# Weight conversion in three phases, and row statistics and reciprocals moved from VectorE to ScalarE and GpSimd, in a top-k attention with an MLP

## The chip, the cores and the metric

The kernel runs on one core of one Trainium2 chip. The metric is device time in microseconds (us). Engines are named as in the profile: PE is TensorE, DVE is VectorE, ACT is ScalarE, POOL is GpSimd and SP is SyncE, which here only issues DMAs. Each engine works through its own instructions in order; waits between engines go by semaphores.

## The reference

Eight batches of eight heads, 576 positions, head width 64. Each row of attention keeps its 32 largest scores; the eight heads' results form rows of 512, which go through a layer norm without bias and a two-layer MLP with a residual.

```python
scores = scale * np.matmul(q, k.transpose(0, 1, 3, 2))
kth = np.partition(scores, -top_k, axis=-1)[..., -top_k:-top_k + 1]
scores = np.where(scores >= kth, scores, -1000000000.0)
attn = np.exp(scores - np.max(scores, axis=-1, keepdims=True))
attn = attn / (np.sum(attn, axis=-1, keepdims=True) + 1e-09)
x = np.matmul(attn, v)            # then (B,H,S,D) -> (B, S, H*D)

mu = np.mean(x, axis=-1, keepdims=True)
var = np.mean((x - mu) ** 2, axis=-1, keepdims=True)
xn = (x - mu) / np.sqrt(var + 1e-06) * g_ln
out = x + np.maximum(xn @ w_ch1, 0.0) @ w_ch2
```

q, k, v and g_ln come as 32-bit floats, the two weight matrices (512 x 2048 and 2048 x 512) as 64-bit floats. The kernel computes in 32 bits.

## The kernel before

**Units and steps.** A unit is 128 query rows of two heads (or the 64 last rows of two heads, a "rest" unit); there are 160. One pass of the loop `for n in range(END)` is a step. In step n different units are at different stages, so that every engine has work: PE makes the scores of unit n+2 and ACT copies them from PSUM (`scores`, `take_scores`, L433 and L414); DVE searches unit n for its 32nd largest score (`select`, L464, L470, L478) and halves unit n+1's rows (`halve`, L456, L457); ACT and POOL mask unit n-1 (`prepare` L490, L491; `mask` L527 on ACT, L530 on POOL), ACT takes its exponential with row sums (`weigh`, L538). Older units are transposed (PE and ACT, L601 to L641, or DVE and DMAs, `move`, L572 to L589) and multiplied with the values (`values`, L664, L672).

**Placing.** When a group's last unit is done, ACT copies the product (`take_values`, L682), PE transposes it, and `place` scales it by the reciprocal of the row sums (`put`, L686, four a group on ACT) into a row tile x. The reciprocal is made on DVE, one instruction for a group (L1350), after the second part of `select`, in the same step before L686. A step in which this happens is called a place step below.

**Blocks.** Two row tiles form a block; there are 18. `Block.stats` runs in the step after x is complete: DVE's two statistics instructions give mean and variance (L737, L738). For the first block DVE also subtracts the mean (L740); for the others POOL negates the mean (L743) and adds it (L746). `inverse` makes the reciprocal root on POOL (L756, and the power L759). PE transposes x (L775), multiplies with the first weight (L821, ACT's relu L844), then with the second (L860 for the first two blocks, L981 with seven products instead of eight for the others, whose sums POOL makes, L911 to L917). ACT evacuates (L946, L955) and scales (L796), POOL adds the residual (L789).

**Filling.** A block's PE work lies in the list `todo`. `fill`, called eight times a step, takes from it as much as a share worked out by `slot` allows, and also runs the delayed work (`Later.settle`, by age in calls of `fill`). `give` puts a new block's items into the list: its transposes stand ahead of the last ten items of the block before. An item is only taken when its condition holds: the transposes want x centred six calls ago.

**Weights.** 32 pieces of 128 x 512 64-bit numbers are fetched by SP (L148) into tiles of a ring of four that x also uses, and turned into 32-bit floats: ACT takes the size and the low word (L164, L166), POOL clamps and takes the sign (L165, L169), DVE shifts (L172), POOL adds (L178). `batches` says which pieces belong to which step: four before the first step, one a step for steps 0 to 7, none in step 8, one in step 9, two a step from 10 to 18, one in 19. For the early pieces the fetch comes a step ahead, the split in the middle of the step, the shift near its end, the join at the end of the next; from step 9 on the fetch comes at the end of the step before, the split in the middle, the shift near the end, the join near the start of the next.

Scratch in PSUM for scores, transposes and value products comes from a ring of five buffers (`brief`).

Of the kernel before, what the change touches and what calls it, by code (L numbers as in the profile page):

```python
# [9 lines left out]
AF = mybir.ActivationFunctionType  # L10
ALU = mybir.AluOpType
FP32 = mybir.dt.float32
# [8 lines left out]
LN_EPS = 1.0e-6  # L21
J = 4
# [7 lines left out]
def compute(  # L30
# [21 lines left out]
    scale = 1.0 / float(D) ** 0.5  # L52
# [4 lines left out]
    def pool(name, bufs, **kw):  # L57
        return ctx.enter_context(tc.tile_pool(name=name, bufs=bufs, **kw))
# [17 lines left out]
    brief_small = pool("brief_small", 2)  # L76
# [36 lines left out]
    columns = const([P, J + NC], "columns")  # L113
    half, gcol = columns[:, 0:J], columns[:, J : J + NC]
    nc.gpsimd.memset(half[:], -0.5)
    w1 = const([P, NC, DFF], "w1")
    w2 = const([P, NF, DM], "w2")
    wt = const([P, 2, NF // 2, 2 * P], "wt")
# [65 lines left out]
    now = [-1]  # L184
# [19 lines left out]
    LATE = NF // 2 + 1  # L204
# [25 lines left out]
    def done(step):  # L230
        return step is not None and step < now[0]

    def pop():
        kind, cost, run, may = todo.pop(0)
        assert not may or may()
        owed[0] -= cost
        run()

    tick = [0]
# [20 lines left out]
            for _, run in due_now:  # L260
                run()

    sums_later, ends_later, stores = Later(), Later(), Later()

    loads, sends = Later(), Later()
    brings = {}
# [1 line left out]
    def fill(least=0):  # L268
        tick[0] += 1
        loads.settle(LOAD_AGE)  # L270
        sends.settle(SEND_AGE)
        ends_later.settle(END_AGE)
        fetch_forms(FETCH_AGE)
# [185 lines left out]
    def select(u, i):  # L459

        nt = range(len(u.tiles))

        def replace(m, t, x):
            nc.vector.match_replace(x, m[:, t, :], x, LOWEST)  # L464

        if i == 1:
            for r in range(low_rounds):
                o = u.low + 8 * r
                for t in nt:
                    nc.vector.max(u.hi[:, t, o : o + 8], u.lo[:, t])  # L470
                if r < low_rounds - 1:
                    for t in nt:
                        replace(u.hi[:, :, o : o + 8], t, u.lo[:, t])
        r0, width = (min(u.low, u.body), HALF + LOWS) if i > 1 else (u.body, HALF)
        pl = brief_small if i in (1, 2) else small
        m = pl.tile([P, 2, 8], FP32, tag=f"m{i}", name=f"m{i}")
        for t in nt:
            nc.vector.max(m[:, t, :], u.hi[:, t, r0 : r0 + width])  # L478
# [242 lines left out]
    class Block:  # L721
# [9 lines left out]
        def stats(self, i):  # L731
            x = self.x[i]
            if self.mv is None:
                self.mv = small.tile([P, 2, 2], FP32, tag="mv", name="mv")
                self.rstd = small.tile([P, 2], FP32, tag="rstd", name="rstd")
            st = brief_small.tile([P, 6], FP32, tag="st", name="st")
            nc.vector.bn_stats(out=st[:], in_=x)  # L737
            nc.vector.bn_aggr(out=self.mv[:, i, :], in_=st[:])  # L738
            if now[0] <= gives_first:
                nc.vector.tensor_scalar_sub(x, x, self.mv[:, i, 0:1])  # L740
            else:
                less = brief_small.tile([P, 1], FP32, tag="less", name="less")
                nc.gpsimd.tensor_scalar(  # L743
                    less[:], self.mv[:, i, 0:1], -1.0, 0.0, ALU.mult, ALU.add
                )
                nc.gpsimd.tensor_scalar(x, x, 1.0, less[:], ALU.mult, ALU.add)  # L746
            self.step[i] = tick[0]

        def centred(self, i):
            return i in self.step and (  # L750
# [3 lines left out]
        def inverse(self):  # L754
            r = self.rstd[:, 0 : self.n]
            nc.gpsimd.tensor_scalar(  # L756
                r, self.mv[:, 0 : self.n, 1], 1.0, LN_EPS, ALU.mult, ALU.add
            )
            nc.gpsimd.tensor_tensor(r, r, half[:, 0 : self.n], ALU.pow)  # L759
            self.ready = True  # L760
# [250 lines left out]
    SEND_AGE, CENTRE_AGE = 1, 6  # L1011
# [38 lines left out]
    def fetch_form():  # L1050
        m = fetched[0]
        k, i = m // 4 % 2, m % 4
        nc.sync.dma_start(
            slot_of(i), scratch[:, k, i].rearrange("p (f n) -> p f n", f=2)
        )
        fetched[0] += 1

    def fetch_forms(age):
        if done(formed[0]):
            free = 4 + sum(tick[0] - x >= age for x in used)  # L1060
            while fetched[0] < min(free, 8 * (len(blocks) - PLAIN)):
                fetch_form()
# [57 lines left out]
    gives = {}  # L1120
# [9 lines left out]
    for j in jobs:  # L1130
        if j.hp == NHP - 1:
            b = j.b
# [26 lines left out]
    def at(i):  # L1159
        return units[i] if 0 <= i < N else None  # L1160
# [42 lines left out]
    def dve_cost(n):  # L1203
        u, ex = at(n), after(n)[0]
        c = 4.0 if u is None else DVE_REST if u.rest else DVE_UNIT
        if n <= CONVERTING:
            c += 1.0
        c += DVE_TURN * (n in turns) + 0.85 * sum(b.n for b in gives.get(n, []))
        return c + DVE_MOVE if ex and ex.moved else c

    def give(n):
# [36 lines left out]
    gives_first = min(gives)  # L1248
    load(fresh[0], nc.sync, nc.scalar)

    nc.scalar.copy(gcol[:], half[:])
    for x in batches[-1]:
        x.fetch()
    turn_heads(fresh[0])
    nc.sync.dma_start(grow[:], g_ln.rearrange("(c p) -> c p", p=P))
    scores(units[0])
# [3 lines left out]
    scores(units[1])  # L1260
    take_scores(units[1])
    load_gain()
    weights(-1, 0)
    weights(-1, 1)
    for n in range(END):
        now[0] = n
# [42 lines left out]
            brings.pop(n)()  # L1309
        if u:  # L1310
            select(u, 0)
        if n > NF // 2:
            join_weights(n)
# [25 lines left out]
        if ex and ex.rest:  # L1339
            keep_den(ex)  # L1340
        if u:
            select(u, 1)
        if moved:
            move(ex)
        if n == gives_first:
# [1 line left out]
                blk.stats(i)  # L1347
        sums_later.settle(SUM_AGE)
        for den in recips.pop(n, []):
            nc.vector.reciprocal(den, den)  # L1350
        if n in turns:
            turn_heads(turns[n])
            later = fresh.index(turns[n]) + 1
# [47 lines left out]
        if n == 0:  # L1401
            for x in batches[-1]:
                x.shift()
            for x in batches[-1][:2]:
                x.join()
        weights(n, 1)
        if 0 < n <= NF // 2:
            join_weights(n)
            for x in batches[-1][n + 1 : n + 2]:
                x.join()  # L1410
        if g and not quick and g.job.hp == NHP - 1:
            for qt in g.qts:
                if qt < J:
# [1 line left out]
        if late and late.job.hp == NHP - 1:  # L1415
            r = late.job.b // 2
# [62 lines left out]
```

## Time and profile before

| | |
|---|---|
| three runs, median | 1562.06 us (1561.92 to 1564.73) |
| the profiled execution's own time | 1566.49 us |
| its span | 1564.6 us |
| granted PE clock, mean | 0.971 |
| busy PE, DVE | 1467.7 us, 1349.1 us |
| busy ACT, POOL | 1075.5 us, 941.2 us |
| bytes moved by DMA | 245.62 MB |

The profile's page lists busy time by engine and the chain of work that ended last. Three kinds of answers from the trace are used beside it: busy time of each engine in a stretch of the span, waits (who waited for whom, us in total, how often, the longest), and groups of equal instructions (line, engine, operation, tiles, shapes, count, then busy us and mean ns of one, then idle time ahead of them and what ended it). A timeline row gives start and duration in us; what stands in brackets is the idle time of the engine ahead of it and what ended that. PE multiplies 32-bit numbers in two records for each product in the program.

### The profile page before, as it was taken

To read this page: it belongs to the slowest core of one execution; us is meant where nothing else is said; L and a number is where in the kernel's file an instruction comes from. 1 tells how busy PE (TensorE), PEld (TensorE's weight loads), DVE (VectorE), ACT (ScalarE), POOL (GpSimd) and SP (SyncE) were. 2 spreads that over 40 slices of the span, in tenths; PEclk is the share of its full clock that TensorE was granted. 3 is DMA by queue.
4 is the path that set the end of the run, shared out by engine and by line. 5 is a ranking of instruction groups with operands and counts; after the bars stand their busy time and mean duration, and the time that the engine had idled before them with its cause. 6 is when DMAs were issued, how large, how long until landed. Compare 5 with 4: busy or idle time off the path is not lost.

```text
span 1564.6 us, 27256 instructions
## 1 busy us (share of the span) xinstructions
PE 1467.7 (94%) x8046; PEld 1108.0 (71%) x8046; DVE 1349.1 (86%) x3873; ACT 1075.5 (69%) x3085; POOL 941.2 (60%) x1302
## 2 busy tenths in 40 slices
PE   3678889999999899999999999999999999999997
PEld 2456447576787677778777777777777777788886
DVE  6998899899889998989988999999999999767000
ACT  5988777786777767777777776867677776554421
POOL 4757776756474666656656556565647475737524
PEclk7789989999999999999999999999999999999998
DMA  6634541567648774686744796666667567464511
GB/s 174 165 100 122 143 114 60 151 157 209 177 127 201 192 204 130 180 207 151 222 119 133 183 225 183 159 171 182 187 173 197 173 173 196 118 173 114 151 35 50
DMA packets 374776, 245.62 MB, mean 157 GB/s; under 512 B 255956, under 2 KB 343512, under 8 KB 374616
## 3 DMA queue, kind: packets, MB, share of 16 engines
q1 hardware_dynamic: 371048, 243.17, 57.9%
q8 instruction: 67, 1.10, 0.3%
q10 hardware_dynamic: 3568, 0.59, 0.3%
q14 instruction: 93, 0.76, 0.2%
HBM read 166.14 MB, written 77.53 MB: 156 GB/s over the span
## 4 chain that ended last, share of the span: by engine, by line
PE 52%; DVE 31%; ACT 5%; DMA 5%; POOL 4%; issue 2%; SPq 1%; DVEq 0%; POOLq 0%; ACTq 0%
PE hps L821 21%; PE ops L981 13%; DVE m L478 10%; DVE hi L464 8%; PE scps L433 6%; PE av L664 5%; DVE sc L572 3%; DVE lo L457 2%; DVE hi L456 2%; PE ops L860 2%; DVE hi L470 2%; PE tp L601 2%; POOL e L530 2%; DMA raw<-in_moe_w_ch_dram 1%; PE av L672 1%
## 5 line engine op out<-in xcount | busy, mean ns | idle before, releaser
L530 POOL TENSOR_TENSOR e<-e,sc 128x576 f32<-128x576 f32 x288 | 408.7, 1437 | 492.6 <-ACT e L527 437.7
L821 PE MATMUL hps<-xT,w 128*128 128x256 f32 x2304 | 542.0, 384 | 1.6 <-ACT xT L781 1.6
L821 PEld LDWEIGHTS hps<-xT,w 128*128 128x128 f32 x2304 | 423.4, 191 | 80.8 <-issue 25.9
L478 DVE MAX8 m<-hi 128x8 f32<-128x296 f32 (+1 forms) x1152 | 472.8, 446 | 1.2
L464 DVE MATCH_REPLACE8 hi<-m,hi 128x288 f32<-128x288 f32 (+1 forms) x864 | 378.0, 443 | 0.0
L981 PE MATMUL ops<-w,h 128*128 128x256 f32 x1280 | 306.9, 385 | 1.3 <-ACT o L946 1.3
L981 PEld LDWEIGHTS ops<-w,h 128*128 128x128 f32 x1280 | 235.0, 191 | 44.8 <-issue 13.4
L414 ACT COPY sc<-scps 128x288 f32<-128x288 f32 x576 | 189.1, 402 | 76.8 <-POOL e L530 56.0
L538 ACT ACTIVATE e<-e,m 128x576 f32<-128x576 f32 x288 | 225.4, 785 | 7.8 <-POOL e L530 5.8
L527 ACT ACTIVATE e<-sc,m 128x576 f32<-128x576 f32 x288 | 209.3, 769 | 0.0
L572 DVE STREAM_TRANSPOSE sc<-e 128x1152 f32<-128x1152 f32 x87 | 119.0, 1367 | 52.7 <-ACT e L538 46.2
L844 ACT ACTIVATE h<-hps 128x512 f32<-128x512 f32 x144 | 86.7, 602 | 111.0 <-PE hps L821 110.4
L664 PE MATMUL av<-pt,vb 128*64 128x256 f32 (+2 forms) x1280 | 150.8, 379 | 9.6 <-DMA pt<-turned 6.2
L664 PEld LDWEIGHTS av<-pt,vb 128*64 128x64 f32 x1280 | 82.2, 142 | 69.6 <-issue 20.7
L456 DVE TENSOR_TENSOR hi<-sc 128x576 f32<-128x576 f32 (+1 forms) x160 | 127.0, 794 | 3.0 <-ACT sc L414 3.0
L457 DVE TENSOR_TENSOR lo<-sc 128x576 f32<-128x576 f32 (+1 forms) x160 | 126.9, 793 | 0.0
L433 PE MATMUL scps<-kT,late_qT 64*128 64x288 f32 (+3 forms) x832 | 119.9, 407 | 0.0
L981 PE MATMUL ops<-wt,s 128*128 128x256 f32 x512 | 119.4, 383 | 0.0
L433 PE MATMUL scps<-kT,qT 64*128 64x288 f32 x512 | 95.1, 465 | 24.6 <-ACT pt L613 9.0
L470 DVE MAX8 hi<-lo 128x8 f32<-128x288 f32 x288 | 117.8, 445 | 0.0
L981 PEld LDWEIGHTS ops<-wt,s 128*128 128x128 f32 x512 | 94.7, 190 | 17.3 <-issue 4.1
L433 PEld LDWEIGHTS scps<-kT,late_qT 64*128 64x128 f32 (+1 forms) x832 | 69.0, 166 | 50.0 <-issue 20.2
(108 smaller groups left out, 1747.2 us busy)
## 6 DMA issues: line engine op xcount, KB each, us to landing
turned<-sc SPq DMA_DIRECT2D x87, 576.0 KB, 4.3
pt<-turned SPq DMA_DIRECT2D x348, 144.0 KB, 3.1
w<-forms SPq DMA_DIRECT2D x128, 256.0 KB, 4.8
vb<-in_v_dram SPq DMA_DIRECT2D x80, 288.0 KB, 4.3
raw<-in_moe_w_ch_dram SPq DMA_DIRECT2D x32, 512.0 KB, 4.7
kT<-kept SPq DMA_DIRECT2D x48, 288.0 KB, 3.8
kept<-kT SPq DMA_DIRECT2D x32, 288.0 KB, 3.7
kqin<-in_k_dram SPq DMA_DIRECT2D x116, 72.0 KB, 2.7
```

Of the source, the lines that this page charges most:

```text
L414: nc.scalar.copy(u.sc[:, t, s * HALF : (s + 1) * HALF], u.made[s][t][:, 0:HALF])
L433: nc.tensor.matmul(ps[i * R : i * R + ql, o : o + width], qT[r, q0 : q0 + ql], kT[r, k0 : k0 + width], start=True, stop=True,)
L456: nc.vector.tensor_tensor(hi, a, b, ALU.max)
L464: nc.vector.match_replace(x, m[:, t, :], x, LOWEST)
L478: nc.vector.max(m[:, t, :], u.hi[:, t, r0 : r0 + width])
L527: nc.scalar.activation(u.e[:, t], u.sc[:, t], AF.Relu, bias=u.edge[:, t : t + 1], scale=-STEEP)
L530: nc.gpsimd.tensor_tensor(u.e[:, t], u.e[:, t], u.sc[:, t], ALU.subtract)
L538: nc.scalar.activation(u.e[:, t], u.e[:, t], AF.Exp, bias=u.bias[:, t : t + 1], scale=-scale, accum_out=g.den[:, col : col + 1],)
L572: nc.vector.transpose(blocks.rearrange("p (j c n) -> p j c n", j=ni, n=32), u.e[:].rearrange("p t n -> p (t n)").rearrange("p (c j k) -> p ...
L664: nc.tensor.matmul(av[h * D : (h + 1) * D, 0 : g.nq], vb[:, h * (J + 1) + c, :], heads_of(g, h, 0, g.nq // 32)[:, :, c], start=(c == 0), s ...
L821: nc.tensor.matmul(ps[0][:, side * N : (side + 1) * N], w1[:, c, f * P : (f + 1) * P], self.xT[:, c, 0:N], start=(c == 0), stop=(c == NC - 1),
L981: nc.tensor.matmul(bank[name][:, 0:Q], a(j), rhs, start=first and j == 0, stop=(j == G - 1), skip_group_check=not first,)
```

## The change

Three things are changed.

1. The conversion has three phases with fixed places in every step. In step n's middle its pieces are fetched, at its end (ahead of the last part of `select`) they are split, and in the middle of step n+1, behind the second part of `select`, they are shifted and joined. Steps 0 to 8 have one piece, 9 to 17 two, 18 one. The four pieces ahead of the loop are joined two in step 0 and two in step 1.
2. Row statistics, except for the first block: ACT copies x with a sum (scale 1/512) into PSUM scratch, POOL negates the sum and adds it to x as before, and six calls of `fill` later ACT squares the centred x with a sum. `inverse` multiplies that sum by 1/512.
3. The reciprocals of the row sums are powers with exponent -1 on POOL. They stand at the same place in the step, which on POOL is behind the masks and, while weights are converted, behind the joins.

```diff
+    minus = half[:, J - 1 : J]
+    nc.gpsimd.memset(minus, -1.0)
...
-        count = 4 if n < 0 else 1 if n < NF // 2 else 0 if n == NF // 2 else 1 + (n > 9)
+        count = 4 if n < 0 else 1 if n <= NF // 2 else 2
...
     def weights(n, phase):
-        now, coming = batches.get(n, []), batches.get(n + 1, [])
-        if phase == 0:
-            for x in coming if n < LATE else []:
+        for x in batches.get(n, []):
+            if phase == 0:
                 x.fetch()
-            for x in now[0::2] if n < LATE else now:
+            elif phase == 1:
                 x.split()
-        elif phase == 1:
-            for x in now[1::2] if n < LATE else []:
-                x.split()
-            for x in coming if n >= LATE else []:
-                x.fetch()
-
-    def join_weights(n):
-        for x in batches.get(n - 1, []):
-            x.join()
+            else:
+                x.shift()
+                x.join()
...
+    def invert(den):
+        nc.gpsimd.tensor_tensor(den, den, minus.to_broadcast(list(den.shape)), ALU.pow)
...
             if now[0] <= gives_first:
+                st = brief_small.tile([P, 6], FP32, tag="st", name="st")
+                nc.vector.bn_stats(out=st[:], in_=x)
+                nc.vector.bn_aggr(out=self.mv[:, i, :], in_=st[:])
                 nc.vector.tensor_scalar_sub(x, x, self.mv[:, i, 0:1])
...
+            self.share = 1.0 / DM
+            less = brief_small.tile([P, 1], FP32, tag="less", name="less")
+            nc.scalar.activation(
+                brief("sum")[:], x, AF.Copy, scale=self.share, accum_out=self.mv[:, i, 0:1]
+            )
+            nc.gpsimd.tensor_scalar(
+                less[:], self.mv[:, i, 0:1], -1.0, 0.0, ALU.mult, ALU.add
+            )
+            nc.gpsimd.tensor_scalar(x, x, 1.0, less[:], ALU.mult, ALU.add)
+
+            def squares():
+                nc.scalar.activation(
+                    brief("squares")[:], x, AF.Square, accum_out=self.mv[:, i, 1:2]
+                )
+
+            squares_later.add(squares)
...
         for den in recips.pop(n, []):
-            nc.vector.reciprocal(den, den)
+            invert(den)
...
+        if n > 0:
+            weights(n - 1, 2)
...
-        for x in batches.get(n, []):
-            x.shift()
+        weights(n, 1)
         if u:
             select(u, 3)
```

In `dve_cost`, the estimate by which `slot` shares out PE work in the first 20 steps, a block's statistics now count for the first block only.

More of the change, by code (lines that the diff above doesn't have):

```diff
@@ L202, in compute @@
     assert not queue
-    LATE = NF // 2 + 1
     def weights(n, phase):
-        now, coming = batches.get(n, []), batches.get(n + 1, [])
-        if phase == 0:
-            for x in coming if n < LATE else []:
+        for x in batches.get(n, []):
+            if phase == 0:
                 x.fetch()
-            for x in now[0::2] if n < LATE else now:
+            elif phase == 1:
                 x.split()
-        elif phase == 1:
-            for x in now[1::2] if n < LATE else []:
-                x.split()
-            for x in coming if n >= LATE else []:
-                x.fetch()
-    def join_weights(n):
-        for x in batches.get(n - 1, []):
-            x.join()
+            else:
+                x.shift()
+                x.join()
     todo = []
@@ L261, in settle @@
                 run()
-    sums_later, ends_later, stores = Later(), Later(), Later()
+    sums_later, ends_later, stores, squares_later = Later(), Later(), Later(), Later()
     loads, sends = Later(), Later()
@@ L272, in fill @@
         ends_later.settle(END_AGE)
+        squares_later.settle(CENTRE_AGE)
         fetch_forms(FETCH_AGE)
@@ L735, in stats @@
                 self.rstd = small.tile([P, 2], FP32, tag="rstd", name="rstd")
-            st = brief_small.tile([P, 6], FP32, tag="st", name="st")
-            nc.vector.bn_stats(out=st[:], in_=x)
-            nc.vector.bn_aggr(out=self.mv[:, i, :], in_=st[:])
+            self.step[i] = tick[0]
             if now[0] <= gives_first:
+                st = brief_small.tile([P, 6], FP32, tag="st", name="st")
+                nc.vector.bn_stats(out=st[:], in_=x)
+                nc.vector.bn_aggr(out=self.mv[:, i, :], in_=st[:])
                 nc.vector.tensor_scalar_sub(x, x, self.mv[:, i, 0:1])
[L741 to L744, printed above, removed]
-                )
-                nc.gpsimd.tensor_scalar(x, x, 1.0, less[:], ALU.mult, ALU.add)
-            self.step[i] = tick[0]
+                self.share = 1.0
+                return
+            self.share = 1.0 / DM
[10 more added lines that the diff above has]
+                    brief("squares")[:], x, AF.Square, accum_out=self.mv[:, i, 1:2]
+                )
+            squares_later.add(squares)
         def centred(self, i):
@@ L756, in inverse @@
             nc.gpsimd.tensor_scalar(
-                r, self.mv[:, 0 : self.n, 1], 1.0, LN_EPS, ALU.mult, ALU.add
+                r, self.mv[:, 0 : self.n, 1], self.share, LN_EPS, ALU.mult, ALU.add
             )
@@ L1207, in dve_cost @@
             c += 1.0
-        c += DVE_TURN * (n in turns) + 0.85 * sum(b.n for b in gives.get(n, []))
+        c += DVE_TURN * (n in turns) + 0.85 * sum(b.n for b in gives.get(n, []) if n == gives_first)
         return c + DVE_MOVE if ex and ex.moved else c
@@ L1251, in compute @@
     nc.scalar.copy(gcol[:], half[:])
-    for x in batches[-1]:
-        x.fetch()
+    weights(-1, 0)
     turn_heads(fresh[0])
@@ L1262, in compute @@
     load_gain()
-    weights(-1, 0)
     weights(-1, 1)
@@ L1311, in compute @@
             select(u, 0)
-        if n > NF // 2:
-            join_weights(n)
         if quick:
             for den in recips.pop(n):
-                nc.vector.reciprocal(den, den)
+                invert(den)
             place(g)
@@ L1349, in compute @@
         for den in recips.pop(n, []):
-            nc.vector.reciprocal(den, den)
+            invert(den)
         if n in turns:
@@ L1403, in compute @@
                 x.shift()
[L1404 to L1410, printed above, removed]
+        for x in batches[-1][2 * n : 2 * n + 2]:
+            x.join()
         if g and not quick and g.job.hp == NHP - 1:
```

## The prediction

> **What bounds the kernel now.** I read the page's head, then the busy time by stretch, the waits, the costs by shape, and the order inside single steps. The profiled execution's own time is 1566.49 us, its span 1564.6; the median of the three runs shown is 1562.06, so 4.4 lower.
>
> ```profile
> span 1564.6 us, 27256 instructions
> PE 1467.7 (94%) x8046; PEld 1108.0 (71%) x8046; DVE 1349.1 (86%) x3873; ACT 1075.5 (69%) x3085; POOL 941.2 (60%) x1302
> ```
>
> PE and DVE are the busy engines. Which of them rules where is seen by stretch (columns: from and to; length; busy PE, PEld, DVE, ACT, POOL; granted clock; DMA share; GB/s).
>
> ```profile
> 46.65:94.85 48.20, 30.82 (x173) 19.50 (x173) 48.20 (x151) 44.45 (x124) 31.86 (x34) 0.79 0.52 144
> 106.10:209.60 103.50, 91.65 (x424) 57.13 (x423) 86.14 (x253) 83.39 (x216) 76.95 (x82) 0.92 0.48 124
> 209.60:245.00 35.40, 30.50 (x140) 19.11 (x139) 35.33 (x107) 25.13 (x68) 21.30 (x22) 0.95 0.27 73
> 245.00:1298.40 1053.40, 1035.70 (x5921) 782.98 (x5921) 1015.33 (x2921) 774.46 (x2288) 642.58 (x908) 1.00 0.65 173
> 1309.65:1564.60 254.95, 243.75 (x1224) 203.49 (x1224) 110.74 (x299) 104.85 (x277) 131.69 (x209) 0.98 0.41 114
> ```
>
> Steps 3 to 8 (46.65 to 94.85) are DVE's, 48.20 of 48.20. In steps 10 to 18 (106 to 210) nobody is full. The middle is nearly DVE's and nearly PE's at once: PE idles 1053.40 - 1035.70 = 17.7 us in it. The tail is PE's alone. DVE's waits that the change touches (us in total, times, longest), and one of the steps in which the last of them falls:
>
> ```profile
> DVE wt L172 <- POOL sign L169: 17.4, 15, 1.3
> DVE size L172 <- POOL sign L169: 5.5, 2, 4.3
> DVE st L737 <- ACT x L686: 36.2, 6, 20.2
> ```
> ```profile
> 418.30:430.10 11.80, 11.80 (x88) 8.46 (x89) 6.46 (x19) 9.32 (x30) 4.43 (x7) 1.00 0.51 148
> ```
>
> The 23 us on POOL's sign are the conversion's. The 36 us on x are worth nothing: the step shown is PE's from end to end (11.80 of 11.80), and the 20.2 lie in the tail.
>
> **The change part by part: prices.**
>
> ```profile
> L737 DVE BATCH_NORM_STATS2 st<-x 128x6 f32<-128x512 f32 x32 | 21.6, 675 | 36.2 <-ACT x L686 36.2
> L738 DVE BATCH_NORM_AGGREGATE mv<-st 128x2 f32<-128x6 f32 x36 | 6.6, 182 | 1.2
> L1350 DVE RECIPROCAL den<-den 128x4 f32<-128x4 f32 x63 | 8.9, 141 | 0.0
> L759 POOL TENSOR_TENSOR rstd<-rstd,columns 128x2 f32<-128x2 f32 x18 | 13.2, 734 | 1.5
> L497 POOL TENSOR_TENSOR watched<-hi,m 128x2 f32<-128x2 f32 x128 | 33.1, 259 | 0.0
> L872 ACT COPY o<-ops 128x512 f32<-128x512 f32 x4 | 2.3, 598 | 1.7 <-PE ops L860 1.7
> L538 ACT ACTIVATION_READ_ACCUMULATOR e<-e,m 128x1 f32 x288 | 57.9, 201 | 0.0
> L796 ACT ACTIVATE o<-o,mv,rstd 128x512 f32<-128x512 f32 x36 | 28.5, 813 | 0.7 <-POOL o L961 0.7
> L1251 ACT ACT_TABLE_LOAD x1 | 1.3, 1283 | 2.9 <-issue 2.9
> ```
> ```profile
> raw<-in_moe_w_ch_dram SPq DMA_DIRECT2D x32, 512.0 KB, 4.7
> ```
>
> DVE loses 34 of 36 statistics (0.675 + 0.182 = 0.86 us a tile, 1.71 a block of two, 29 in all) and 80 reciprocals (0.14 each, 11): 40 us of 1349.
>
> ACT gains 34 sums and 34 squares. The trace has neither. A pass with its accumulator read lies between 0.70 (copy 0.598 and read 0.201, 0.1 of it overlapped) and 1.01 (0.813 + 0.201); I take 0.8, the copy being nearest: 54 us, 3.2 a block. Each also takes a turn of the five PSUM buffers that scores and transposes use; that is free while ACT reaches the pass in time, else PE waits for the buffer. POOL's L743 now waits for ACT's sum instead of DVE; ACT sums right behind its own L686, so not later, and what stands behind L743 (centring, the next masks) is no worse off.
>
> POOL gains 80 powers. Two columns cost 0.734, a plain operation of that shape 0.259. Four columns cost 0.73 if the power's price is fixed, 0.259 + 2 x 0.475 = 1.21 if it goes by column. I take 1.2, because the power's own share, not the start, is the larger part: 64 x 1.2 + 16 x 0.73 = 88 us. The conversion's operations keep their number.
>
> The Trainium skill (GPSIMD Engine Reference, section 4.1) puts GpSimd about 2x behind VectorE in elementwise work. By that a power would be 0.28, an estimate, and the place steps of term 1 would lose 0.9 each. The trace has 5x (734 against 141), and the measurement decides.
>
> **Term 1, steps 0 to 8: +6.** A step in which a group is placed (L686, which reads the reciprocals), with the split in its middle:
>
> ```profile
> 62.88 0.21 ACT L490 ACTIVATE m<-m 128x2 f32<-128x2 f32 x1 [0.45 <-DVE m L478]
> 65.61 0.71 ACT L164 ACTIVATE size<-raw 128x512 f32<-128x512 f32 x1
> 66.20 0.67 ACT L166 ACTIVATE wt<-raw 128x512 f32<-128x512 uint32 x1
> 68.19 0.20 ACT L538 ACTIVATION_READ_ACCUMULATOR e<-e,m 128x1 f32 x1
> 69.06 0.93 ACT L686 ACTIVATE x<-xo,den 128x64 f32<-128x64 f32 x4
> 70.33 0.31 ACT L641 COPY pt<-tp 128x128 f32<-128x128 f32 x1
> 71.09 0.21 ACT L490 ACTIVATE m<-m 128x2 f32<-128x2 f32 x1 [0.45 <-DVE m L478]
> ```
> ```profile
> 63.97 2.85 POOL L530 TENSOR_TENSOR e<-e,sc 128x576 f32<-128x576 f32 x2 [2.47 <-ACT e L527]
> 68.38 1.33 POOL L178 TENSOR_TENSOR w<-size,wt 128x512 uint32<-128x512 uint32 x1
> ```
>
> ACT has 0.45 us to spare in 8.21. Today the split pair (65.61 to 66.87, 1.26) fills time in which ACT would half wait for the second mask; at the step's end nothing covers it. Counted from L490: masks end at +3.94 (66.82), the second exponential at +4.85, ACT stands at L686 at +5.6. POOL by then must do the watch (to +4.1), the join (1.3) and, behind it, the power (1.2): +6.6. From L686 to L641's end stays 1.58, so +8.2; the pair makes +9.4. That is +1.2 in steps 3, 5 and 7; steps without a place come out even. In the first of them DVE has no lead yet and the join waits for its shift: +1. At the start DVE's 5.5 us of waits go, but ACT keeps its order and one more split stands on POOL ahead of step 2's masks: +1.5. Behind the waiting L686 are L613, L641 and the split, hence the next masks: ACT and POOL rule these steps then, DVE no longer. SP's fetch moves too; its buffer comes free with L169 near a step's start and the split comes most of a step later, which hides the 4.7 us to landing; uncovered, it would hold ACT at L164.
>
> **Term 2, steps 9 to 18, two pieces each: -4.5.**
>
> ```profile
> 175.35 0.21 ACT L490 ACTIVATE m<-m 128x2 f32<-128x2 f32 x1 [3.14 <-DVE m L478]
> 181.84 0.95 ACT L686 ACTIVATE x<-xo,den 128x64 f32<-128x64 f32 x4
> 184.23 0.20 ACT L550 ACTIVATE den<-den 128x4 f32<-128x4 f32 x1
> 186.88 0.21 ACT L490 ACTIVATE m<-m 128x2 f32<-128x2 f32 x1 [2.45 <-DVE m L478]
> ```
> ```profile
> 179.39 2.52 POOL L178 TENSOR_TENSOR w<-wt 128x512 uint32<-128x512 uint32 x2
> ```
>
> Today's loop takes 11.53 us (186.88 - 175.35): masks, joins and splits on POOL, then shift and last maximum on DVE, then ACT and the masks again. The change opens it. ACT's place step becomes: POOL's watch to +4.1, joins 2.5, power 1.2, so L686 at +7.85; 2.6 to L550's end; two pairs 2.4: 12.9. The step between has no place: ACT's 9.1 (175.35 to 184.43) less 1.0 for L686 and L682, plus a relu, 8.8. A pair of steps takes 21.7 against 23.06, 0.65 a step, -6 over nine steps; I keep -4.5, since PE is already 89% busy there at a granted 0.92.
>
> **Term 3, steps 19 to 22: -3.** DVE is full (35.33 of 35.40), PE idles 4.9. DVE sheds 1.71 and comes in ahead of ACT, which with 25 busy of 35 catches up.
>
> **Term 4, the middle: -12.5.** DVE's relief pays where PE runs dry:
>
> ```profile
> 368.10:379.00 10.90, 8.55 (x44) 5.92 (x43) 10.83 (x32) 5.42 (x16) 8.34 (x14) 0.84 0.71 201
> 541.60:552.40 10.80, 8.97 (x46) 6.24 (x45) 10.73 (x31) 5.58 (x17) 6.96 (x11) 0.84 0.75 214
> 939.10:950.00 10.90, 9.14 (x54) 6.62 (x52) 10.83 (x32) 6.12 (x17) 7.05 (x11) 1.00 0.75 226
> 1298.40:1309.20 10.80, 8.01 (x53) 5.40 (x49) 10.73 (x31) 6.22 (x19) 5.86 (x8) 1.00 0.71 193
> ```
>
> Each holds a block's statistics; DVE is full, PE has 2.35, 1.83, 1.76 and 2.79 to spare. With the relief that DVE gathers since PE last ruled (1.71 here, 0.14 for each reciprocal, and a block before) they give 2.9, 1.8, 1.8 and 2.8. Of the other 9 us that PE idles I count a third, 3.2. ACT is busy 774 of 1053, over 125 steps 2.2 us idle each, which covers 3.2 a block; uncovered, its evacuations come late and PE with them. Ends: 3 and 17.7.
>
> **Term 5, the tail: +3.9.** In the changed order nine of the former block's products leave step 148 and stand behind the new block's transposes: `give` holds the last ten items back, and the list is then no longer than ten. PE rules from there.
>
> ```profile
> 1529.27 24.19 PE ops L981 x112
> ```
>
> 0.216 a record, two records a product: 9 x 0.43 = 3.9.
>
> **Sum:** 6 - 4.5 - 3 - 12.5 + 3.9 = -10.1. The profiled 1566.49 becomes 1556.4, the median 1552.
>
> **The rivals.** (a) ACT does not come to rule steps 2 to 18, the power being short: 5.5 at the start, PE's 11.9 idle in 106 to 210, and 3 after it are all won: -20.4 - 12.5 + 3.9 = -29, 1533. For it: DVE waits there for POOL alone. Against: ACT's 44.45 of 48.20. (b) No change: PE rules the middle, 98% busy, and term 4 is 3: -0.6, 1561. Against: the four steps above. (c) Slower: the power takes the reciprocal's place on the path. In POOL's queue behind joins or a block's sums it holds ACT at L686 in all 64 place steps; this decides once it and the new passes exceed ACT's 2.2 us a step. Then term 1 is 9, terms 2 and 4 nothing: 9 - 3 + 3.9 = +9.9, 1572. (d) The squares need another table set: 68 loads of 1.283 are +87, 1649. Against: the changed program holds one load a pass, as before.
>
> The Trainium skill (ScalarE: Activation LUTs, "Table sets: the hidden batching unit") names relu, copy, identity and abs as in every set, not square, and asks about 2.7 us a switch, 182 in all by its price. No run here shows a switch.
>
> **How the numbers follow.** Forecast 0.55, (a) 0.15, (b) 0.14, (c) 0.15, (d) 0.01. Two per mille, 3.1 us, is about what a measurement tells from no change; so faster 0.70, same 0.14, slower 0.16. The likeliest is 1552; alone it spans 1544 to 1558 (term 4 between 6.5 and 17.7, the rest 3 either way). Leaving out no more than 0.2, the range reaches into (a) and (c): 1535 to 1567.
>
> **What would show it.** Right: no DVE wait on L169 between 106 and 210; ACT waiting at L686 for the power there; steps 3, 5 and 7 longer than 8.2; powers near 1.2; busy DVE near 1309, ACT 1130, POOL 1029; PE idle under 8 in the middle; ten products behind the transposes of step 149. Wrong: powers over 2 us or under 0.5, ACT waits at L686 in the middle, PE waiting for buffers that the sums hold, new dips of the granted clock.

## The result and the profile after

The changed kernel takes 1586.53 us in the median of five runs (1582.2 to 1589.13), the kernel before 1562.06 (five runs beside it, 1560.09 to 1564.87): 1.015 times as long, 95% interval 1.0135 to 1.0165. The prediction was 1552 with a range of 1535 to 1567. The change makes the kernel slower, by more than the range allowed.

The page's head, then the costs by shape, of the changed kernel (columns as in the prediction; behind the bar busy time, mean ns of one, idle time before):

```profile
span 1584.7 us, 27372 instructions
...
PE 1484.0 (94%) x8046; PEld 1115.9 (70%) x8046; DVE 1336.3 (84%) x3725; ACT 1113.8 (70%) x3221; POOL 1041.2 (66%) x1383
```
```profile
L640 POOL TENSOR_TENSOR den<-den,columns 128x4 f32<-128x4 f32 x64 | 69.6, 1088 | 0.0
...
L640 POOL TENSOR_TENSOR dr<-dr,columns 128x2 f32<-128x2 f32 x16 | 11.8, 740 | 0.0
...
L741 ACT ACTIVATE sum<-x 128x512 f32<-128x512 f32 x30 | 18.0, 602 | 0.0
...
L741 ACT ACTIVATION_READ_ACCUMULATOR sum<-x 128x1 f32 x30 | 6.0, 201 | 0.0
...
L174 DVE SCALAR_TENSOR_TENSOR wt<-wt,sign 128x512 uint32<-128x512 uint32 x20 | 26.6, 1357 | 1.2 <-POOL sign L171 1.2
...
L174 DVE SCALAR_TENSOR_TENSOR size<-size,sign 128x512 uint32<-128x512 uint32 x12 | 13.3, 1124 | 3.9 <-POOL sign L171 3.7
```

The prices of the new work came out as taken: the power 1.09 us for 1.2, a statistics pass 0.60 + 0.20 for 0.8. DVE's waits for POOL's sign (23 us before) are 5. But the shifts, L172 before and L174 now, take 1357 and 1124 ns where they took 688 and 833. They stood like this in the kernel before:

```profile
L172 DVE SCALAR_TENSOR_TENSOR wt<-wt,sign 128x512 uint32<-128x512 uint32 x20 | 13.8, 688 | 17.4 <-POOL sign L169 17.4
...
L172 DVE SCALAR_TENSOR_TENSOR size<-size,sign 128x512 uint32<-128x512 uint32 x12 | 9.7, 833 | 5.5 <-POOL sign L169 5.5
```

By stage (steps 3 to 8, 10 to 18, 19 to 22, the middle from step 23 to 147, and from step 149 on; columns as before). A step counts from here on from DVE's first search in it; the prediction's stretch of steps 19 to 22, 35.40 us, begins 1.4 us ahead of that, and counted like the others it is 33.9:

```profile
42.80:101.20 58.40, 38.39 (x182) 24.20 (x181) 54.55 (x152) 49.24 (x139) 42.74 (x41) 0.70 0.46 130
117.20:221.40 104.20, 91.19 (x422) 57.34 (x423) 103.04 (x249) 80.92 (x212) 88.48 (x87) 0.94 0.48 129
221.40:256.10 34.70, 32.07 (x140) 20.74 (x138) 32.93 (x99) 26.90 (x76) 19.08 (x20) 0.88 0.17 43
256.10:1310.30 1054.20, 1037.98 (x5918) 782.10 (x5918) 991.69 (x2812) 802.82 (x2387) 718.45 (x973) 0.99 0.65 174
1319.10:1584.70 265.60, 250.25 (x1246) 207.79 (x1242) 101.47 (x282) 114.06 (x308) 137.08 (x216) 0.98 0.38 110
```

The middle is as long as before, 1054.20 us for 1053.40, though DVE is 24 us less busy in it. What is new stands in the waits (of the changed kernel, the whole span first, then steps 10 to 18: total, times, longest):

```profile
ACT x L681 <- POOL den L640: 31.5, 10, 5.0
...
POOL less L744 <- ACT sum L741: 29.7, 7, 11.8
...
PEld scps L425 <- ACT x L681: 20.6, 9, 5.1
...
PE scps L425 <- ACT x L681: 16.2, 7, 4.7
```
```profile
ACT x L681 <- POOL den L640: 19.3, 4, 5.0
...
PE scps L425 <- ACT x L681: 12.4, 4, 4.7
```

L681 is the scaling that was L686, L640 the power. One of the longest of the ten is in step 24. Its timeline (start, length, what, in brackets the idle time before and its releaser):

```profile
263.68 1.28 POOL L1041 TENSOR_TENSOR wt<-w 128x512 f32<-128x512 f32 x1
...
265.04 1.27 POOL L1042 TENSOR_TENSOR wt<-w,wt 128x512 f32<-128x512 f32 x1
...
266.27 2.49 POOL L796 TENSOR_TENSOR o<-o,x 128x512 f32<-128x512 f32 x2
...
268.72 1.01 POOL L640 TENSOR_TENSOR den<-den,columns 128x4 f32<-128x4 f32 x1
...
269.77 0.93 ACT L681 ACTIVATE x<-xo,den 128x64 f32<-128x64 f32 x4 [4.96 <-POOL den L640]
...
270.34 2.21 PE L425 MATMUL scps<-kT,late_qT 64*128 64x288 f32 x6 [2.88 <-ACT x L681]
...
272.47 1.44 ACT L519 ACTIVATE e<-sc,m 128x576 f32<-128x576 f32 x2
...
275.12 1.57 DVE L448 TENSOR_TENSOR hi<-sc 128x576 f32<-128x576 f32 x1 [5.23 <-ACT sc L406]
```
```profile
263.70:277.40 13.70, 10.82 (x39) 7.76 (x38) 8.47 (x25) 7.97 (x25) 10.04 (x10) 0.77 0.00 1
```

The same stretch, parted at the end of PE's stop:

```profile
263.70:270.30 6.60, 3.77 (x19) 2.65 (x17) 6.19 (x22) 1.64 (x6) 5.96 (x6) 1.00 0.00 0
270.30:277.40 7.10, 7.06 (x20) 5.12 (x21) 2.28 (x3) 6.33 (x20) 4.08 (x4) 0.55 0.00 1
```

POOL is hardly idle here: two differences of weights (L1041, L1042) and two residual sums (L796), 5 us of work, stand ahead of the power. ACT stands 4.96 us at L681. The products for scores wait for L681 (they write the PSUM buffer that it reads), so PE stops for 2.88 us between two of them. The granted clock is 1.00 up to there and 0.55 in the 7.1 us behind it. The scores are late, and DVE waits 5.23 us for them. The step is 4.3 us longer than step 24 before (13.70 against 9.37), and 6.1 longer than in the kernel with everything but the power (7.60, e1 below), over a power of 1.01 us. The stop and what the lowered clock takes (7.1 us at 0.55, so 3.2 us, an estimate) make about these 6.1.

**A measure for the rest.** PE executes the same matmuls in every kernel here, in another order. Its work at full clock is worked out from the records as 0.844 ns a column (the prediction's 0.216 us for 256 columns), and half of that for products of 64 rows or 64 columns, which overlap in pairs (16 of 256 columns took 1.95 us in e7, 0.122 each); an estimate, it sums to 1344.6 us before and after. A stretch's length less PE's work in it is PE's excess: idle time, lowered clock and small gaps. The excess of a kernel and 1344.6 give its span, so stages can be compared though products wander between them:

| excess, us | before | changed | weights only | no power | plan as before | power early | tail on DVE |
|---|---|---|---|---|---|---|---|
| start to end of step 9 | 73.7 | 83.4 | 77.2 | 79.6 | 79.3 | 80.3 | 78.9 |
| steps 10 to 18 | 27.2 | 27.7 | 17.7 | 18.3 | 20.0 | 18.8 | 19.4 |
| steps 19 to 22 | 10.5 | 10.2 | 7.3 | 8.2 | 7.5 | 8.5 | 9.1 |
| steps 23 to 148 | 90.0 | 93.9 | 93.0 | 82.7 | 79.0 | 85.6 | 82.9 |
| step 149 to the end | 18.6 | 24.7 | 16.8 | 25.1 | 23.7 | 22.7 | 17.4 |
| all | 220.0 | 240.1 | 212.1 | 214.0 | 209.6 | 215.7 | 207.8 |

The five columns on the right are the experiments e3, e1, e5, e7 and e9. These are single profiled executions, which differ from the medians by up to 4.4 us; a difference under 2 us in one row is not read.

### The profile page after: what moved, and what is told of

Its sections match the earlier page's. It is cut to its first block, busy times and chain, and to the rows that moved or that the text cites. A ratio compares the mean times of both kernels' runs of the same rounds, so it can differ in the third digit from the quotient of the medians.

```text
span 1584.7 us, 27372 instructions
## 1 busy us (share of the span) xinstructions
PE 1484.0 (94%) x8046; PEld 1115.9 (70%) x8046; DVE 1336.3 (84%) x3725; ACT 1113.8 (70%) x3221; POOL 1041.2 (66%) x1383
## 5 line engine op out<-in xcount | busy, mean ns | idle before, releaser
L522 POOL TENSOR_TENSOR e<-e,sc 128x576 f32<-128x576 f32 x288 | 417.2, 1467 | 382.4 <-ACT e L519 326.0
L406 ACT COPY sc<-scps 128x288 f32<-128x288 f32 x576 | 188.2, 402 | 85.6 <-POOL e L522 66.7
L530 ACT ACTIVATE e<-e,m 128x576 f32<-128x576 f32 x288 | 225.4, 784 | 18.4 <-POOL e L522 16.2
L519 ACT ACTIVATE e<-sc,m 128x576 f32<-128x576 f32 x288 | 209.3, 768 | 0.0
L425 PE MATMUL scps<-kT,late_qT 64*128 64x288 f32 (+3 forms) x832 | 127.4, 413 | 9.3 <-ACT x L681 7.0
L449 DVE TENSOR_TENSOR lo<-sc 128x576 f32<-128x576 f32 (+1 forms) x160 | 127.6, 798 | 0.0
L425 PEld LDWEIGHTS scps<-kT,late_qT 64*128 64x128 f32 (+1 forms) x832 | 71.9, 168 | 62.8 <-issue 18.3
```

Of the source, the lines that this page charges most:

```text
L406: nc.scalar.copy(u.sc[:, t, s * HALF : (s + 1) * HALF], u.made[s][t][:, 0:HALF])
L425: nc.tensor.matmul(ps[i * R : i * R + ql, o : o + width], qT[r, q0 : q0 + ql], kT[r, k0 : k0 + width], start=True, stop=True,)
L449: nc.vector.tensor_tensor(lo, a, b, ALU.min)
L519: nc.scalar.activation(u.e[:, t], u.sc[:, t], AF.Relu, bias=u.edge[:, t : t + 1], scale=-STEEP)
L522: nc.gpsimd.tensor_tensor(u.e[:, t], u.e[:, t], u.sc[:, t], ALU.subtract)
L530: nc.scalar.activation(u.e[:, t], u.e[:, t], AF.Exp, bias=u.bias[:, t : t + 1], scale=-scale, accum_out=g.den[:, col : col + 1],)
```

## The experiments

The theory to begin with, P: the power stands in POOL's queue behind other work, ACT waits for it at the scaling, and PE and DVE with it. Rivals: W, the weights' new phases lose the time (the slow shifts); F, the altered costs of the plan reorder PE's products to no good. Times are medians; ratios are to the kernel before, run beside each, whose median lies between 1562.06 and 1564.5 us.

**e1, the reciprocals back on DVE.**

```
 def invert(den):
-    nc.gpsimd.tensor_tensor(den, den, minus.to_broadcast(list(den.shape)), ALU.pow)
+    nc.vector.reciprocal(den, den)
```

> The changed kernel with its 80 reciprocals back on DVE; weights and statistics stay as changed. Theory P (the power stands in POOL's queue behind joins, LayerNorm sums and the like, ACT stands at the scaling of x for it, PE then runs out of scores and its clock falls): the 31.5 us that ACT waits for den and the 37 us that PE waits for ACT's scaling go; step 24 falls from 13.7 back to about 9.4 us, PE's slack in steps 23 to 27 from 9.8 to about 2.5; in all 15 to 22 us less than the changed kernel, 1565 to 1572. Theory W (the weights' new phases are the loss: shifts on DVE slowed from 0.69 to 1.36 us): at most 5 us less, 1582 or more. Theory F (the loss comes with the reordered products that the altered costs give): at most 3 us less.

1558.99 us, 0.997 (0.9959 to 0.9981). Taking the power away gains 27.5 us, more than P gave (15 to 22), and the rest of the change is then a small gain over the kernel before. W and F fall as main causes. (The 37 us in the expectation add the waits of weight loads, 20.6, to those of matmuls, 16.2, which run side by side; PE's own stops are the 16.2.) The wait at L681 for the reciprocal is small:

```profile
ACT x L681 <- DVE den L640: 6.0, 4, 1.8
```

Of the 26.1 us between the two profiled executions, the table puts 11.2 into steps 23 to 148, 9.4 into steps 10 to 18, 3.8 up to step 9 and 2.0 into steps 19 to 22: the difference of the columns changed and no power.

**e2, the statistics back on DVE; e3, the weights' phases alone; e4, all but the weights' phases.** e2 takes `stats` and `dve_cost` of the kernel before into the changed one; e3 does that and e1's edit; e4 puts the new `stats`, `dve_cost` and `invert` into the kernel before.

> The changed kernel with the row statistics back on DVE, their cost in the plan too; weights and powers stay as changed. Theory P: the power's waits stay and the relief of DVE (29 us of its time, of which PE got about 10) is lost: 5 to 12 us more than the changed kernel, 1592 to 1598. Theory F: the products come back to their former order, so 5 to 12 us less, 1575 to 1581. If ACT's passes held ACT up by as much as DVE gained: no difference.

> The kernel before with the weights' new phases alone (pieces split at a step's end, shifted and joined in the next; batches one step later); reciprocals and statistics as before. Theory P: steps 0 to 9 lose up to 5 us and steps 10 to 22 come out between 0 and 4 us shorter: 1560 to 1567. Theory W: 10 us or more over the kernel before, 1572 or more, nearly all of it before 250 us.

> The kernel before with the statistics on ACT and the power for the reciprocals; the weights' phases as before. Theory P: the loss of the power stays (15 to 22 us), the relief of DVE too (10 us), the weights' share of the loss (up to 7 us before 250 us) is gone: 1566 to 1577. Theory W: about 1552 to 1562, the loss being gone with the phases.

e2: 1580.67, 1.0109 (1.0093 to 1.0125). e3: 1561.36, 0.9986 (0.9977 to 0.9996). e4: 1589.02, 1.016 (1.0143 to 1.0178). The weights' phases gain about 2 us without the power (e3), and with it no loss is seen (e4 to the changed kernel, 2.5 us, where the intervals overlap). e4 missed both of its forecasts by 12 us or more: they took the phases for a part of the loss or for all of it, and they are none.

e2's expectation failed in sign: 1592 to 1598 was expected, on the argument that DVE's relief goes; it is 6 us faster than the changed kernel, inside what theory F gave (1575 to 1581). The power costs 19 us with DVE's statistics (e3 to e2) and 27.5 with ACT's. Where e2 is faster is seen by parting the span at the start of step 148, first e2, then the changed kernel:

```profile
0.00:1312.50 1312.50, 1225.31 (x6773) 905.48 (x6775) 1247.48 (x3471) 966.02 (x2791) 889.30 (x1159) 0.97 0.61 163
1312.50:1577.50 265.00, 251.73 (x1275) 209.43 (x1271) 120.24 (x323) 111.03 (x296) 146.81 (x224) 0.98 0.42 118
```
```profile
0.00:1310.20 1310.20, 1226.86 (x6773) 904.28 (x6775) 1225.97 (x3419) 992.85 (x2894) 898.29 (x1159) 0.96 0.61 164
1310.20:1584.70 274.50, 257.14 (x1277) 211.59 (x1273) 110.37 (x307) 120.95 (x328) 142.88 (x224) 0.97 0.40 114
```

From step 148 on, ACT's statistics and their plan's cost lose 9.5 us (265.0 to 274.5); without the power they lose 10.3 there (264.4 in e3 to 274.7 in e1). The expectation had nothing for this, and it is what e5 and e9 take apart. Ahead of step 148 the statistics gain 2.3 us with the power and 8.3 without it (1292.3 to 1284.0). Why the power leaves so little of that gain was not tried. POOL's wait of 29.7 us for ACT's sums does not explain it: e1 has 32.4 us of the same wait, and 22.3 of the 29.7 are two waits in steps 150 and 159.

**e5, the plan's cost as before.** e1's kernel, and

```
-        c += ... + 0.85 * sum(b.n for b in gives.get(n, []) if n == gives_first)
+        c += ... + 0.85 * sum(b.n for b in gives.get(n, []))
```

> The kernel of the run without powers (reciprocals on DVE, statistics on ACT, the weights' new phases), and the plan's cost of a step as in the kernel before, which counts the statistics of every block. PE's program is then again the one with the products ahead of the last block's transposes. Theory O (the loss behind step 147, 8 us more from step 148 to the end than with DVE's statistics, is the order of PE's products): the stretch from the start of step 148 to the end falls from 274.7 to about 267, 1550 to 1554 in all. Rival: the loss is ACT's sums and squares in the way of evacuations: the time stays at 1557 to 1561.

1556.05, 0.9946 (0.9929 to 0.9963), between what O and its rival gave, and the interval just touches e1's. PE's products are now in the order of e3 throughout, and from step 145 on in that of the kernel before. The edit of one cost had held back two products near step 20 and shifted the list, and nine products fell behind the last transposes. Steps 148 and 149, first without the power (e1), then with the plan as before (e5):

```profile
1284.00:1292.90 8.90, 5.56 (x35) 2.99 (x31) 8.90 (x28) 6.76 (x21) 4.84 (x8) 1.00 0.78 218
1292.90:1301.70 8.80, 6.48 (x23) 5.71 (x24) 8.80 (x27) 5.04 (x15) 2.80 (x3) 0.61 0.44 136
```
```profile
1284.70:1293.50 8.80, 8.80 (x52) 5.99 (x53) 8.80 (x27) 7.21 (x22) 5.26 (x7) 1.00 0.82 220
1293.50:1302.30 8.80, 7.13 (x40) 5.70 (x37) 8.80 (x27) 6.31 (x19) 4.15 (x5) 1.00 0.57 165
```

PE has 15.9 us busy in place of 12.0, and in step 149 the granted clock is 1.00 in place of 0.61. From the start of step 148 to the end it is 269.5 us against 274.7, not the 267 expected: as the weights alone take 264.4, half of the loss is something else. e4, whose products stand in the order of the kernel before, loses there too (273.3 us for 266.2). A part of it is seen in e5's step 157:

```profile
1404.95 0.37 ACT L953 COPY o<-ops 128x256 f32<-128x256 f32 x1 [8.44 <-DMA out_dram<-o]
...
1405.22 0.61 ACT L741 ACTIVATE sum<-x 128x512 f32<-128x512 f32 x1
...
1405.84 0.59 ACT L741 ACTIVATE sum<-x 128x512 f32<-128x512 f32 x1
...
1405.99 1.32 PE L425 MATMUL scps<-kT,late_qT 64*128 64x288 f32 x2 [2.37 <-ACT sum L741]
```

ACT stands 8.44 us at a copy whose target a store still reads. The sums behind it have a PSUM buffer in their turn, and PE, which needs it for scores, stops.

**e6, the power besides.** e1's kernel, and at each reciprocal POOL raises as many columns of a constant to the power as well; nothing reads the result.

> The kernel of the run without powers, and at the place of each reciprocal POOL raises as many columns to a power besides, with a result that nothing reads: POOL's load is that of the changed kernel, but nobody waits for the power. Theory P1 (the loss is ACT's wait for den at the scaling of x and what follows): 1558 to 1564. Theory P2 (the loss is POOL's time: masks behind the power come late): 1574 or more, most of the 27 us of the changed kernel. Between them, the share of each can be read.

1559.94, 0.998 (0.9971 to 0.9989), within 1 us of e1 and its interval, with POOL as busy as in the changed kernel (1042.6 us against 1041.2). Its 80 us of POOL cost nothing that these runs can tell:

```profile
L643 POOL TENSOR_TENSOR st<-columns 128x4 f32<-128x4 f32 x64 | 68.7, 1074 | 0.0
```

P2, POOL's load, falls; what costs is that somebody waits.

**e7, the powers at the head of the step.** The changed kernel, with

```
+        for den in recips.pop(n, []):
+            invert(den)
         if quick:
             values(g)
...
         sums_later.settle(SUM_AGE)
-        for den in recips.pop(n, []):
-            invert(den)
```

and the same for the `quick` steps. **e8** is e7 with e5's cost.

> The changed kernel with the powers issued at the head of the step, ahead of its masks in POOL's queue; the reciprocals' inputs stand ready there since the step before. Theory P1: ACT's wait for den (31.5 us) falls under 5 and most of the 27 us go: 1560 to 1570. Theory P2: the masks come 1.1 us late instead: 1580 or more.

> As the run with the powers at the head of the step, and the plan's costs as in the kernel before, so PE's products in the former order. Theory O: 6 to 10 us under that run. Rival: the same time as that run, within 3 us.

e7: 1563.11, 0.9995 (0.9987 to 1.0004); e8: 1558.2, 0.9967 (0.9957 to 0.9977). The same 80 powers at the same price (1083 ns), issued earlier, cost 4 us where they cost 27.5. The wait for den is gone from L681:

```profile
L640 POOL TENSOR_TENSOR den<-den,columns 128x4 f32<-128x4 f32 x64 | 69.3, 1083 | 0.0
...
L681 ACT ACTIVATE x<-xo,den 128x64 f32<-128x64 f32 x256 | 58.7, 311 | 8.0 <-PE xo L704 7.6
```

and a power at the step's head lies where POOL would wait for ACT's exponent argument (L519) anyway, so it holds the mask behind it back by little. That mask starts as the power ends, at 262.18, some 0.6 us behind the first of the two L519:

```profile
260.67 1.53 POOL L640 TENSOR_TENSOR den<-den,columns 128x4 f32<-128x4 f32 x1
...
260.81 1.44 ACT L519 ACTIVATE e<-sc,m 128x576 f32<-128x576 f32 x2
...
262.18 2.79 POOL L522 TENSOR_TENSOR e<-e,sc 128x576 f32<-128x576 f32 x2
```

So 23 of the 27 us are the power's place in the queue. The order of the products is worth 5 us here (e7 to e8), under the 6 to 10 of theory O and over its rival's 3.

**e9, the statistics from step 147 on by DVE.** On e5:

```
-            if now[0] <= gives_first:
+            if now[0] <= gives_first or now[0] >= 147:
                 st = brief_small.tile([P, 6], FP32, tag="st", name="st")
                 nc.vector.bn_stats(out=st[:], in_=x)
```

with the centring left on POOL there.

> As the run with the plan's costs of before (reciprocals on DVE, the weights' new phases, statistics on ACT), with the statistics from step 147 on back on DVE, where PE rules and DVE has time. Theory A (in the tail ACT's sums stand behind evacuations that wait for a store, and hold PE's buffer): PE's slack from step 149 to the end falls from 23.7 to about 17, the 2.4 us that PE waits for the sum go, and the time falls by 4 to 6 us, to 1550 to 1552. Rival: the stall at step 157 is the store's own and stays: within 2 us of 1556.

1551.4, 0.9918 (0.9903 to 0.9934): 4.7 us under e5, where the intervals just touch, and the excess from step 149 on is 17.4 for 23.7. From step 148 on it is 265.0 us, as in the kernels with DVE's statistics. So ACT's statistics in the tail are the other half of its loss. PE's wait for the sum is gone. The copy itself still waits for its store (8.2 us at the longest), as the rival had it, but no sum stands behind it now. That wait was 2.4 us of PE's; what else the statistics held up in the tail was not traced.

**e10, shift and join behind the third selection; e11, this and e9.** On e5 and e9:

```
-        if n > 0:
-            weights(n - 1, 2)
...
         if u:
             select(u, 2)
+        if n > 0:
+            weights(n - 1, 2)
```

> As the run with the plan's costs of before, with shift and join behind the third selection of the step and not behind the second. Theory X (a DVE instruction with two inputs and a POOL mask or join exclude each other, 1.89 us in place of 0.68): at the new place POOL has its masks done, the shift falls to 0.7 to 0.9 us, the mask's L522 to under 1.45, DVE is 8 to 14 us less busy. What that is worth: in steps 3 to 8, where DVE is full, up to 1.2 us a step; in steps 10 to 18 up to 2 us a step if DVE rules them, nothing if ACT and POOL rule: 1545 to 1555. Rival Y: the shift is slow for another reason and stays at 1.1 us: no difference. Against both, the later join may hold the next masks: up to 5 us slower.

> Both of the last two edits. If they are independent, their differences add: 1541 to 1552 by theories A and X, 1556 by their rivals.

e10: 1552.58, 0.9932 (0.9917 to 0.9947). e11: 1548.76, 0.9907 (0.9891 to 0.9923), the fastest kernel here: 0.9% under the kernel before, and about what e9's and e10's differences from e5 add up to (1547.9). The shift falls to 684 ns as theory X has it, but DVE is no less busy (1342.2 us against e5's 1338.4), and steps 10 to 18 take 98.0 us against 98.6. The time went to the next instructions of the same kind. Costs by shape over steps 10 to 18, first e5, then e10:

```profile
L174 DVE SCALAR_TENSOR_TENSOR wt<-wt,sign 128x512 uint32<-128x512 uint32 x18 | 20.7, 1187 | 0.0
...
L449 DVE TENSOR_TENSOR lo<-sc 128x576 f32<-128x576 f32 x9 | 10.4, 1157 | 0.0
...
L448 DVE TENSOR_TENSOR hi<-sc 128x576 f32<-128x576 f32 x9 | 7.6, 848 | 0.0
```
```profile
L174 DVE SCALAR_TENSOR_TENSOR wt<-wt,sign 128x512 uint32<-128x512 uint32 x18 | 11.6, 685 | 0.0
...
L449 DVE TENSOR_TENSOR lo<-sc 128x576 f32<-128x576 f32 x10 | 17.2, 1718 | 0.0
...
L448 DVE TENSOR_TENSOR hi<-sc 128x576 f32<-128x576 f32 x9 | 10.1, 1126 | 0.0
```

9.1 us less in the shifts, 8.5 more in the two halves, which now meet the joins (one of e10's ten L449, of 0.75 us, belongs to the step ahead). e10's 3.5 us against e5 are within what the intervals leave open.

## Why the prediction was wrong, by its steps

**What bounds the kernel: right.** PE and DVE in the middle, PE in the tail, DVE's waits for POOL's sign up to step 18.

**Prices: right** for the power, the passes and DVE's relief. (The 5x in them sets a power of two columns against a reciprocal of four; like for like it is 1088 against 141, 7.7x. And 68 switches at the price cited come to 184, not 182.) Two forecasts of busy time held (POOL 1029, measured 1041.2; ACT 1130, measured 1113.8), DVE's did not (1309, measured 1336.3): 16.4 us of the difference are the shifts, which the prediction let move at their old duration; the other 10.9 were not traced.

**Term 1, +6: the size held, the place in part.** The start to step 8 is 4.9 us longer (101.2 for 96.3). Steps 3, 5 and 7 take 10.2, 9.7 and 8.4 us, over the 8.2 named. But steps 4, 6 and 8, said to come out even, take 10.5, 9.8 and 9.8 for 8.15, 8.15 and 7.55, and step 9, counted with term 2, 15.96 for 11.36. Without the power the start to step 8 is 98.5, with the weights alone 97.1: somewhat over half of it is the power. Two of ACT's waits for the power, 1.80 and 1.26 us, fall at 55.16 and 73.44, when DVE has already begun steps 4 and 6; so a part of a place step's loss is counted in the step behind it.

**Term 2, -4.5: the mechanism right, the power's part wrong.** The loop opens. Alone, the weights' phases take steps 10 to 18 from 103.5 to 98.1 us; DVE is then full and the clock is 0.99 for 0.92 (the stretch in e3):

```profile
111.00:209.10 98.10, 90.15 (x433) 56.28 (x433) 98.10 (x253) 85.52 (x222) 88.05 (x86) 0.99 0.52 138
```

The term set the place step to 12.9 us and the other to 8.8; with the power they are 11.5 and 12.0 in the middle of the stage (steps 14 and 15), together 23.4 as before, for the 21.7 forecast. ACT waits there at L681 as was foreseen, 19.3 us in four steps, yet PE's stop behind it, 12.4 us, was not in the term. The gain of 5 became a loss of 0.8.

**Term 3, -3: near without the power.** Steps 19 to 22 take 31.3 us in e1 for 33.9 before, 34.7 in the changed kernel.

**Term 4, -12.5: the step that failed.** For the statistics it was right: from the weights alone to the kernel without power the excess of steps 23 to 148 falls from 93.0 to 82.7, by 10.3. But the term had nothing for the power in these steps, on the ground that DVE's reciprocals are relieved and ACT has 2.2 us to spare a step. In the runs the power took 11.2 back. PE's idle time, forecast under 8, is 16.2 (1054.20 - 1037.98). The reasoning compared totals a step; the wait comes from single steps, like step 24, in which POOL's queue holds 5 us ahead of the power. In the middle these are six waits in steps 24, 26, 64, 66, 67 and 91, 12.9 us of ACT's together, and step 24 alone is 6.1 us longer than without the power. The prediction's own signs of being wrong named both things that came, ACT's waits in the middle and a new dip of the clock. (Of the four steps of this term the last is step 148, outside the 17.7 us that PE idles in the middle; so the rest was 11.8 and not 9.)

**Term 5, +3.9: right in its cause, half of its size.** The nine products do move, and cost about what was said (e1 to e5: 3 us in the medians, 5.2 from step 148 on). A further 5 us in the tail is ACT's statistics (e5 to e9). The prices named this condition for ACT's passes, free while ACT reaches the pass in time, else PE waits for the buffer; the tail, where ACT stands behind stores, was not looked at for it.

**The rivals.** (c) is what happened: the power in POOL's queue behind other work holds ACT. It had 0.15 and +9.9, 1572; the profiled spans differ by 20.1. By its own terms: term 1 was 9 (9.7 with step 9), terms 2 and 4 nothing (0.5 and 3.9), term 3 -3 (-0.3), term 5 3.9 (6.1). The medians differ by 4.4 more, since the profiled execution of the kernel before was that much over its median. So each of its stages was within 4 us, and their sum was half of what came; its chance was too low, and the range ended below it. That ACT is held in all 64 place steps fell: it was ten waits (31.5 us), and three more at the two-column powers (5.9). (a) and (b) are out by the result; (d) by 34 squares at 0.6 us and one table load in the whole span.

The Trainium skill (SBUF — State Buffer, "Who interferes with whom") states that a VectorE instruction with two SBUF inputs contends with a GpSimd instruction that reads SBUF, and calls the port pair that they share an exclusive lock. The traces agree (0.68 us became 1.90 for a shift that met a mask), and it was the rule to weigh against the moved shift. In the weights-only kernel, the shifts and masks that meet:

```profile
114.77 2.53 DVE L174 SCALAR_TENSOR_TENSOR wt<-wt,sign 128x512 uint32<-128x512 uint32 x2
```
```profile
114.91 3.66 POOL L522 TENSOR_TENSOR e<-e,sc 128x576 f32<-128x576 f32 x2
```

Two shifts take 2.53 us for twice 0.68 in e10, two masks 3.66 for 2.79 in e7: each side waits for the other.

## What to carry to other kernels

An operation that moves to a busy in-order queue is priced by its place in that queue in the worst steps, not by its duration or the engine's spare time: the same powers cost 27 us behind other work, 4 us issued early, and 1 us, which is within the noise, when nobody waited for them. When a wait is followed, follow it to the end: what stands behind the waiting instruction on its engine, which buffer that keeps, and whether PE then stops long enough to lose its clock. And a cost in a planner is part of the change: two products held back near step 20 were worth 3 us in the tail.

## What the runs showed of the hardware

VectorE's shift and GpSimd's mask, which both read two operands from SBUF, ran nearly one after the other (two of each took 2.53 and 3.66 us for 1.36 and 2.79), and the time lost is handed on: taken from the shift (9.1 us), it came back in the next such instructions that met POOL's (8.5 us), with no change of the stage's length beyond the noise (98.6 to 98.0).

A stop of PE of 2.88 us was followed by a granted clock of 0.55 over the next 7.1 us, which took about 3.2 us more; so a stop costs more than its own length. No threshold follows from these traces: in the kernel before a stop of 1.93 us (at 1136.8) is followed by 0.50, and one of 3.34 us (at 509.5) by 1.00.
